# When weight splits and a difference of x are made at the end of an opening block, in an FNet and GLU kernel

## The chip, the core and the metric

The kernel runs on one core of a Trainium2 chip. TensorE (PE) multiplies matrices, VectorE (DVE) and ScalarE (ACT) work on elements, GpSimd (POOL) issues the storing transfers here and does a few tiny operations, SyncE (SP) issues the loading transfers. Each engine takes its instructions in the order in which they are written. The metric is the device time of one execution in microseconds; the median of several executions is compared.

## The reference

`x` is 2048 x 512 (S x D), F is 1792.

```python
xn = layernorm(x)                                # over D
a = xn @ dft_hid_re.T;  b = xn @ dft_hid_im.T
s = dft_seq_re @ a - dft_seq_im @ b              # real part of a 2-D DFT
h = sigmoid(xn @ w_gate) * (xn @ w_up)           # 2048 x 1792
g = silu(h @ w_down)
return x + s * g
```

Everything is float32. The kernel keeps that accuracy by splitting each operand into two float32r parts, hi (a rounded copy, made by ACT) and lo (the value less hi, made by DVE); a product is then three matmuls, hi x hi, hi x lo and lo x hi (`mm3`, lines 72 to 75). Every operand of a product thus costs an ACT copy and, after it, a DVE subtraction (`split`, lines 68 to 70) before TensorE may use it.

## The kernel before

The F dimension is taken in seven groups `g` of 256, the rows of x in two halves `h` of 1024. For a half and a group the gate and up products are made by a scheme of seven products with sums of quarters (Strassen's, in Winograd's form) in place of eight: products 1, 2, 3 and 4 use plain quarters on one side or both, the others use sums on both. The products run in the order 1, 5, 2, 6, 7, 4, 3, and each is one unit of the list `units`: 12 matmuls 128x512 per product, and in some units 12 more (bank `pd`) for the down projection of the group before. `xop[h, k]` is the x operand of product k and `w[k]` the weight operand, both as hi and lo. For product 5 the weight operand is the sum `s1` and the x operand is `x_sum(h, 1)`, a difference of two transposed blocks; for product 6 the weight operand is `s2`, made from `s1`, and the x operand is `x_sum(h, 2)`, made from the first difference. `x_sum(h, 3)` and `x_sum(h, 4)` serve products 7 and 4.

The first group of the first half (h = 0, g = 0) is not done so. It is the opening block, `start` (line 504): its eight plain products run in `chunk(q, f)`, q = 0 to 3 outside and f = 0, 1 inside, while the eight tiles of x are still normalised, turned by TensorE (`turn`) and split (`keep_hi` on ACT, `keep_lo` on DVE) or kept plain (`keep_raw` on ACT). A chunk is 24 matmuls of 256 columns, eight each on hi x hi, and the two mixed pairs. `next_tile(7)`, the last tile, stands inside chunk (2, 1), and chunk (3, 0) is the first that uses it. `gated(b, f)` makes a gated value from two finished banks (ACT sigmoid line 544, DVE multiply line 545); the function it returns, kept in `left`, splits that value one chunk later. Behind the opening block come the units: unit 0 is product 1 of group 1, unit 1 product 5 with, after it, the first down projection of the opening block, for which the weights `w_down[0]` are split in two parts; unit 2 is product 2 and unit 3 product 6.

The order is written out by hand. The opening block calls `units[n][0][1].get()` for n = 0 to 3 (line 624), which makes and splits the weights of products 1, 5, 2 and 6 ahead of their units, one each in chunks (1, 1), (2, 0), (2, 1) and (3, 0). From unit 0 on, the main loop (lines 974 to 986) asks for the operands of a unit two units ahead (`SPLIT_AHEAD`) and for loads five units ahead; `sooner` and `after` hang further work in front of a unit or behind it.

All of it lives in 53 buffers named `page`. A buffer is given again once its last reader is through, so a load into a page waits for whoever used that page before. SP issues its loads in order: a load that waits holds the next ones.

Of the kernel before, what the change touches and what calls it, by code (L numbers as in the profile page):

```python
# [32 lines left out]
def fnet_glu_kernel(ctx: ExitStack, tc: tile.TileContext, x, x_t, c_re, c_im, w_h, w_gu, w_down, out):  # L33
# [9 lines left out]
    def page(shape, dtype=F32R):  # L43
        return pages.tile([P, *shape], dtype, name="page")

    def bank(tag):
        return banks.tile([P, 512], F32, name=tag, bufs=2 if tag == "pd" else 1)
# [77 lines left out]
    xop = {}  # L125
    xraw = {}
    units = []
# [7 lines left out]
    def after(n, f):  # L135
        extra.setdefault(n, []).append(f)
# [7 lines left out]
    def fetch(i, hold=False):  # L144
        pg = page([2, D], F32)
        if hold:
            nc.vector.memset(pg[:, 0, :1], 0.0)
        for j in range(2):
            xs[i + j] = pg[:, j, :]
            nc.sync.dma_start(xs[i + j], x[(i + j) * P : (i + j + 1) * P, :])  # L150
# [3 lines left out]
    def norm_a(i):  # L154
        st = stat.tile([P, 6], F32, name="st")
        mv = stat.tile([P, 2], F32, name="mv")
        rs = stat.tile([P, 2], F32, name="rs")
        nc.vector.bn_stats(st, xs[i])
        nc.vector.bn_aggr(mv, st)
        mean, scale = mv[:, 0:1], rs[:, 1:2]  # L160
        if i >= KH:
            mean, scale = (moments[:, m, i - KH : i - KH + 1] for m in range(2))
            nc.gpsimd.tensor_scalar(mean, mv[:, 0:1], 0.0, None, op0=ALU.add)
        nc.gpsimd.tensor_scalar(rs[:, 0:1], mv[:, 1:2], EPS, None, op0=ALU.add)
        nc.gpsimd.tensor_tensor(scale, rs[:, 0:1], mhalf, op=ALU.pow)
        st_of[i] = mean, scale

    def norm_b(i):
        mean, scale = st_of.pop(i)
        nc.vector.tensor_scalar(xs[i], xs[i], mean, scale, op0=ALU.subtract, op1=ALU.mult)  # L170
# [30 lines left out]
    def turn(i):  # L201
        turned[i] = bank("pd").rearrange("p (d s) -> p d s", d=ND)
        for d in range(ND):
            nc.tensor.transpose(turned[i][:, d, :], xs[i][:, d * P : (d + 1) * P], ident)
# [5 lines left out]
    def keep_raw(i):  # L210
        keys, at = place(i)
        for j, k in enumerate(keys):
            if k not in xraw:
                xraw[k] = page([2, SB], F32)
            nc.scalar.activation(xraw[k][:, :, at], turned[i][:, 2 * j : 2 * j + 2, :], AF.Copy)

    def keep_hi(i):
        keys, at = place(i)
        for j, (h, _, b) in enumerate(keys):
            k = h, XK[j, b]  # L220
            if xop[k].at is None:
                xop[k].at = page([2, SB]), page([2, SB])
            nc.scalar.activation(xop[k].at[0][:, :, at], turned[i][:, 2 * j : 2 * j + 2, :], AF.Copy)

    def keep_lo(i):
        keys, at = place(i)
        for j, (h, _, b) in enumerate(keys):
            hi, lo = xop[h, XK[j, b]].at
            nc.vector.tensor_tensor(lo[:, :, at], turned[i][:, 2 * j : 2 * j + 2, :], hi[:, :, at].bitcast(F32), op=SUB)
# [3 lines left out]
    def x_sum(h, k):  # L233

        if (h, k) not in xsum:
            xsum[h, k] = page([2, SB], F32)
        a, b = {
            1: lambda: (xraw[h, 0, 1], xraw[h, 0, 0]),
            2: lambda: (xraw[h, 1, 1], xsum[h, 1]),
            3: lambda: (xraw[h, 1, 1], xraw[h, 0, 1]),  # L240
            4: lambda: (xraw[h, 1, 0], xsum[h, 2]),
        }[k]()
        nc.vector.tensor_tensor(xsum[h, k], a, b, op=SUB)
# [260 lines left out]
    def start(h, g):  # L504

        loads = [Load(w_gu[g, k], [2, 4 * P]) for k in range(2)]
        wdl = Load(w_down[g], [2, D])
        wd = [Parts([wdl], lambda f=f: wdl.load()[:, f, :], [D], joint=True) for f in range(2)]
        w, ps = {}, {}
        job = Ready(h, g, wd)  # L510

        def w_hi(f, j):
            k, o = QUAD[f, j]
            both = page([2, 4 * P])
            w[f, j] = both[:, 0], both[:, 1]
            nc.scalar.activation(both[:, 0], loads[k].load()[:, o, :], AF.Copy)

        def w_lo(f, j):
            k, o = QUAD[f, j]
            nc.vector.tensor_tensor(w[f, j][1], loads[k].load()[:, o, :], w[f, j][0].bitcast(F32), op=SUB)  # L520

        def chunk(q, f, order, between=None):
            b, a = divmod(q, 2)
            if a == 0:
                for m in range(2):
                    ps[b, f, m] = bank("gu"[m] + ("bc", "ab")[b][f])
            at = slice(a * 2 * P, (a + 1) * 2 * P)
            for n, (u, v) in enumerate(order):
                if n and n - 1 in (between or {}):
                    between[n - 1]()  # L530
                for j, m, k in itertools.product(range(2), repeat=3):
                    d, o = 2 * j + k, (2 * m + k) * P
                    nc.tensor.matmul(
                        ps[b, f, m][:, at],
                        w[f, j][u][:, o : o + P],
                        xop[h, XK[j, b]].at[v][:, k, at],
                        start=n == d == a == 0,
                        stop=n == 2 and d == ND - 1,
                        skip_group_check=True,
                    )  # L540

        def gated(b, f):
            s = page([SB], F32)
            nc.scalar.activation(s, ps[b, f, 0], AF.Sigmoid)
            nc.vector.tensor_mul(s, s, ps[b, f, 1])

            def fin():
                v = job.hs[f, b] = Parts([], lambda: s, [SB], joint=True)
                v.get()

            return fin

        def begin():
            idle = bank("gc")

            def busy(times, wide):
                for _ in range(times):
                    nc.tensor.matmul(idle[:, :wide], ones[:, :P], ones[:, :wide], start=True, stop=True)

            busy(10, 512)  # L560
            fetch(0)
            loads[0].load()
            norm_a(0)
            fetch(2, hold=True)
            loads[1].load()
            norm_a(1)
            w_hi(0, 0)
            norm_b(0)
            turn(0)
            busy(2, 256)  # L570
            keep_hi(0)
            norm_b(1)
            turn(1)
            busy(4, 256)
            keep_hi(1)
            w_hi(0, 1)
            w_lo(0, 0)
            norm_a(2)
            for i in (4, 6):
                fetch(i, hold=True)  # L580
            for n in range(4):
                units[n][0][1].load()
            wdl.load()
            w_lo(0, 1)
            for i in range(2):
                keep_lo(i)
            w_hi(1, 0)
            w_hi(1, 1)
            norm_b(2)
            for i in range(2):  # L590
                keep_raw(i)
            norm_a(3)
            w_lo(1, 0)
            w_lo(1, 1)
            norm_b(3)

            def next_tile(i):
                if i >= KH:
                    return
                turn(i)  # L600
                keep_hi(i)
                if 3 < i + 1 < KH - 1:
                    norm_b(i + 1)
                keep_lo(i)
                if i + 2 < KH:
                    norm_a(i + 2)
                keep_raw(i)

            left = None
            for q in range(4):  # L610
                for f in range(2):
                    if f == 0:
                        chunk(q, f, ((0, 0), (1, 0), (0, 1)))
                        next_tile(2 * q + 2)
                    else:
                        chunk(q, f, ((0, 0), (0, 1), (1, 0)), {int(q == 0): lambda: next_tile(2 * q + 3)})
                    if left:
                        left()
                    left = gated(q // 2, f) if q % 2 else None
                    if (q, f) == (1, 1):  # L620
                        norm_b(KH - 1)
                    n = 2 * q + f - 3
                    if 0 <= n < 4:
                        units[n][0][1].get()
            left()
            x_sum(h, 1)
            x_sum(h, 2)
            after(0, lambda: x_sum(h, 3))
            after(0, lambda: x_sum(h, 4))

        return job, begin

# [312 lines left out]
    with tc.manual_schedule():  # L945
# [3 lines left out]
        for h in range(NH):  # L949
            for g in range(1 - h, NG):  # L950
                job = block(h, g, job, Seven(h, g) if h else Plain(h, g))
            if h == 0:
                n = len(units)
# [85 lines left out]
```

## Time and profile before

| | |
|---|---|
| runs shown | 825.22, 827.76 and 1164.65 us, median 827.76 us |
| profiled execution, own time | 823.7 us |
| its span, first to last instruction | 821.9 us |
| PE busy | 808.8 us, 98% of the span |
| DVE, ACT, POOL busy | 77%, 59%, 18% |
| mean granted TensorE clock | 0.997 |

The span leaves 1.8 us of the profiled execution's time outside it. The run of 1164.65 us is far from the other two, which lie 2.5 us apart. In the rows of the timeline a line number such as L69 is the line of a helper, so operations are told apart by their place in the order: L69 and L70 are the two halves of every split, L223, L229 and L215 are `keep_hi`, `keep_lo` and `keep_raw`, L121 is a sum of weights, L243 an `x_sum`, L533 a chunk's matmul.

### The profile page before, as it was taken

What the parts mean: (1) busy time and instruction counts of PE and PEld (TensorE: products, weight loads), DVE (VectorE), ACT (ScalarE), POOL (GpSimd) and SP (SyncE); (2) the same over time, 40 slices, a digit from 0 to 9 for tenths busy, and PEclk for the clock granted to TensorE, in tenths of its full rate; (3) what the DMA queues carried; (4) which work ended last, traced back from release to release, by engine and by line L of the source; (5) the groups of instructions that cost most, each with busy time, mean ns of one, the idle gap of its engine ahead of it and who ended that gap; (6) DMA issues with size and microseconds to landing.
All of it is one profiled execution on the core that took longest, in us unless ns stands there. A gap on an engine that the chain in (4) does not pass through costs nothing.

```text
span 821.9 us, 10340 instructions
## 1 busy us (share of the span) xinstructions
PE 808.8 (98%) x3654; PEld 671.5 (82%) x3654; DVE 636.5 (77%) x792; ACT 486.4 (59%) x740; POOL 147.5 (18%) x222
## 2 busy tenths in 40 slices
PE   9889999999999999999999999999999999999997
PEld 7868888888888888888888888888888888888786
DVE  6768668768878767766788797889888976997946
ACT  4555555556676787787787774444354545535441
POOL 3123552121111221212121110011101110002201
PEclk9999999999999999999999999999999999999999
DMA  8247999996767899999999897458937994799984
GB/s 298 86 158 274 221 323 254 336 274 170 221 147 209 241 231 246 247 194 228 272 292 303 185 359 281 147 205 306 315 145 286 333 393 152 250 323 399 312 265 77
DMA packets 58660, 204.64 MB, mean 249 GB/s; under 512 B 6640, under 2 KB 6896, under 8 KB 58608
## 3 DMA queue, kind: packets, MB, share of 16 engines
q0 software_dynamic: 24624, 85.48, 41.2%
q1 hardware_dynamic: 33984, 118.50, 40.9%
q8 instruction: 28, 0.46, 0.2%
q14 instruction: 24, 0.20, 0.1%
HBM read 121.63 MB, written 85.99 MB: 253 GB/s over the span
## 4 chain that ended last, share of the span: by engine, by line
PE 94%; DVE 3%; ACT 1%; issue 1%; POOL 0%; DVEq 0%
PE pd L73 6%; PE pd L75 6%; PE pd L74 6%; PE ga L73 5%; PE ua L73 5%; PE ga L74 5%; PE ua L74 5%; PE ua L75 5%; PE ga L75 5%; PE gc L74 3%; PE uc L73 3%; PE gc L75 3%; PE uc L74 3%; PE uc L75 3%; PE gc L73 3%; PE gb L74 3%
## 5 line engine op out<-in xcount | busy, mean ns | idle before, releaser
L70 DVE TENSOR_TENSOR page<-page 128x1024 fp32r<-128x1024 f32 (+1 forms) x362 | 340.5, 969 | 134.4 <-ACT page L69 133.4
L69 ACT ACTIVATE page<-page 128x1024 fp32r<-128x1024 f32 (+1 forms) x362 | 291.4, 853 | 112.1 <-DVE page L121 77.4
L121 DVE TENSOR_TENSOR page<-page 128x1024 f32<-128x1024 f32 (+2 forms) x184 | 169.3, 934 | 1.9 <-PE ua L74 1.4
L302 ACT ACTIVATE page<-pd 128x512 f32<-128x512 f32 x154 | 90.6, 597 | 85.1 <-PE pd L75 78.5
L306 POOL DMA_DIRECT2D g_part<-page x69 | 60.5, 911 | 271.2 <-ACT page L302 169.6
L73 PE MATMUL pd<-page 128*128 128x512 f32 x242 | 94.3, 389 | 0.8 <-DVE page L883 0.8
L75 PE MATMUL pd<-page 128*128 128x512 f32 x242 | 94.2, 389 | 0.0
L74 PE MATMUL pd<-page 128*128 128x512 f32 x242 | 94.1, 389 | 0.0
L73 PE MATMUL ga<-page 128*128 128x512 f32 x200 | 78.0, 390 | 0.0
L74 PE MATMUL ga<-page 128*128 128x512 f32 x200 | 77.8, 389 | 0.0
L73 PE MATMUL ua<-page 128*128 128x512 f32 x200 | 77.8, 389 | 0.0
L75 PE MATMUL ga<-page 128*128 128x512 f32 x200 | 77.8, 389 | 0.0
L74 PE MATMUL ua<-page 128*128 128x512 f32 x200 | 77.8, 389 | 0.0
L75 PE MATMUL ua<-page 128*128 128x512 f32 x200 | 77.8, 389 | 0.0
L73 PEld LDWEIGHTS pd<-page 128*128 128x128 f32 x242 | 45.4, 188 | 10.6 <-issue 1.2
L75 PEld LDWEIGHTS pd<-page 128*128 128x128 f32 x242 | 45.4, 188 | 9.5
L74 PEld LDWEIGHTS pd<-page 128*128 128x128 f32 x242 | 45.4, 188 | 9.4
L73 PE MATMUL gc<-page 128*128 128x512 f32 x124 | 48.6, 392 | 2.3 <-ACT page L69 2.3
L74 PE MATMUL gc<-page 128*128 128x512 f32 x124 | 48.6, 392 | 0.8 <-DVE page L70 0.8
L73 PE MATMUL ub<-page 128*128 128x512 f32 (+1 forms) x126 | 48.3, 383 | 0.5 <-DVE page L925 0.5
L73 PE MATMUL uc<-page 128*128 128x512 f32 x124 | 48.7, 393 | 0.0
L75 PE MATMUL gc<-page 128*128 128x512 f32 x124 | 48.6, 392 | 0.0
(130 smaller groups left out, 1314.1 us busy)
## 6 DMA issues: line engine op xcount, KB each, us to landing
g_part<-page POOLq DMA_DIRECT2D x77, 512.0 KB, 9.0
page<-f_part SPq DMA_DIRECT2D x36, 512.0 KB, 5.7
page<-in_c_re_dram SPq DMA_DIRECT2D x34, 512.0 KB, 6.4
page<-in_c_im_dram SPq DMA_DIRECT2D x33, 512.0 KB, 6.8
page<-in_w_gu_dram SPq DMA_DIRECT2D x28, 512.0 KB, 6.5
f_part<-page POOLq DMA_DIRECT2D x28, 512.0 KB, 6.6
page<-in_w_down_dram SPq DMA_DIRECT2D x14, 512.0 KB, 7.1
page<-xn_part SPq DMA_DIRECT2D x14, 512.0 KB, 8.0
```

What stands on the lines that cost most here:

```text
L69: nc.scalar.activation(hi, src, AF.Copy)
L70: nc.vector.tensor_tensor(lo, src, hi.bitcast(F32), op=SUB)
L73: nc.tensor.matmul(ps, ws[0], ms[0], start=first, stop=False, skip_group_check=go_on)
L74: nc.tensor.matmul(ps, ws[0], ms[1], start=False, stop=False, skip_group_check=go_on)
L75: nc.tensor.matmul(ps, ws[1], ms[0], start=False, stop=last, skip_group_check=go_on)
L121: (engine or nc.vector).tensor_tensor(dst, a, b, op=op)
L302: nc.scalar.activation(pg[:, o, :], po, AF.Copy, scale=float(sign))
L306: nc.gpsimd.dma_start(g_part[i], pg, accum_op=ADD)
```

## The change

```diff
                     else:
                         chunk(q, f, ((0, 0), (0, 1), (1, 0)), {int(q == 0): lambda: next_tile(2 * q + 3)})
+                    if (q, f) == (3, 0):
+                        x_sum(h, 1)
+                    if (q, f) == (3, 1):
+                        xop[h, 5].get()
                     if left:
                         left()
                     left = gated(q // 2, f) if q % 2 else None
@@
                     n = 2 * q + f - 3
                     if 0 <= n < 4:
-                        units[n][0][1].get()
+                        units[(0, 2, 1, 3)[n]][0][1].get()
             left()
-            x_sum(h, 1)
             x_sum(h, 2)
             after(0, lambda: x_sum(h, 3))
-            after(0, lambda: x_sum(h, 4))
+            after(1, lambda: x_sum(h, 4))
```

The weights of product 2, which are plain, are split in chunk (2, 0), and those of product 5, a sum, in chunk (2, 1): the two change places. The first difference of x is made after chunk (3, 0) and split after chunk (3, 1), ahead of the gated value (1, 0); before, it was made after the last gated value was split, and its split stood in unit 0. The fourth difference moves from the end of unit 0 to the end of unit 1. No operation is added or taken away, and TensorE's order stays as it is.

On ACT, from the split of the gated value (0, 1) on, the order before is this. page_181 and page_183 hold the plain weights of group 1, page_447 their sums; page_400, page_516 and page_550 are gated values.

```order
L69 ACTIVATE page_444<-page_400 128x512
L69 ACTIVATE page_449<-page_447 128x512 [waits DVE_49]
L223 ACTIVATE page_331<-pd_462 128x2x128 [waits PE_49]
L223 ACTIVATE page_334<-pd_462 128x2x128
L215 ACTIVATE page_347<-pd_462 128x2x128 [waits DVE_49]
L215 ACTIVATE page_349<-pd_462 128x2x128
L69 ACTIVATE page_489<-page_181 128x512
L544 ACTIVATE page_516<-ga_407 128x512 [waits PE_49]
L69 ACTIVATE page_520<-page_447 128x512 [waits DVE_49]
L69 ACTIVATE page_547<-page_516 128x512
L544 ACTIVATE page_550<-gb_452 128x512 [waits PE_49]
L69 ACTIVATE page_553<-page_550 128x512 [waits DVE_49]
```

The row behind these is the split of the first difference of x, 128x1024. In the changed kernel, where page_487 holds the sums, page_516 the first difference and page_518 and page_556 the gated values, the same stretch reads:

```order
L69 ACTIVATE page_444<-page_400 128x512
L69 ACTIVATE page_447<-page_181 128x512
L223 ACTIVATE page_331<-pd_460 128x2x128 [waits PE_49]
L223 ACTIVATE page_334<-pd_460 128x2x128
L215 ACTIVATE page_347<-pd_460 128x2x128 [waits DVE_49]
L215 ACTIVATE page_349<-pd_460 128x2x128
L69 ACTIVATE page_489<-page_487 128x512 [waits DVE_49]
L544 ACTIVATE page_518<-ga_407 128x512 [waits PE_49]
L69 ACTIVATE page_522<-page_487 128x512 [waits DVE_49]
L69 ACTIVATE page_549<-page_516 128x1024
L69 ACTIVATE page_553<-page_518 128x512
L544 ACTIVATE page_556<-gb_450 128x512 [waits PE_49]
```

The copy that waits for DVE's sum stands behind the last tile's `keep_hi` and `keep_raw` instead of ahead of them, and the copy of the first difference stands ahead of the last two gated values.

On DVE, from the multiply of the gated value (1, 0) on, before; page_185 is `w_down[0]`:

```order
L545 TENSOR_TENSOR page_516<-page_516,ua_408 128x512
L121 TENSOR_TENSOR page_447<-page_447,page_181 128x512
L70 TENSOR_TENSOR page_520<-page_447,page_520 128x512
L70 TENSOR_TENSOR page_547<-page_516,page_547 128x512
L545 TENSOR_TENSOR page_550<-page_550,ub_453 128x512
L70 TENSOR_TENSOR page_553<-page_550,page_553 128x512
L243 TENSOR_TENSOR page_556<-page_347,page_197 128x1024
L243 TENSOR_TENSOR page_558<-page_349,page_556 128x1024
L70 TENSOR_TENSOR page_561<-page_556,page_560 128x1024
L70 TENSOR_TENSOR page_564<-page_185,page_564 128x512
L70 TENSOR_TENSOR page_567<-page_185,page_567 128x512
```

and in the changed kernel, from the first difference on:

```order
L243 TENSOR_TENSOR page_516<-page_347,page_197 128x1024
L545 TENSOR_TENSOR page_518<-page_518,ua_408 128x512
L121 TENSOR_TENSOR page_487<-page_487,page_181 128x512
L70 TENSOR_TENSOR page_522<-page_487,page_522 128x512
L70 TENSOR_TENSOR page_550<-page_516,page_549 128x1024
L70 TENSOR_TENSOR page_553<-page_518,page_553 128x512
L545 TENSOR_TENSOR page_556<-page_556,ub_451 128x512
L70 TENSOR_TENSOR page_559<-page_556,page_559 128x512
L243 TENSOR_TENSOR page_562<-page_349,page_516 128x1024
L70 TENSOR_TENSOR page_564<-page_185,page_564 128x512
L70 TENSOR_TENSOR page_567<-page_185,page_567 128x512
```

The lo part of the first difference (page_561 before, page_550 now) is written five places sooner against the gated values, and the two splits of `w_down[0]` stay last in the row, right behind the second difference.

Since pages are given out in the order in which they come free, some loads get another page than before. SP's loads of the later tiles of x and of the weights that follow wait before for this:

```order
L150 DMA page_773<-in_x_dram 128x512 [waits DMAHW4_49,DMAHW2_49,DVE_49]
L150 DMA page_773<-in_x_dram 128x512 [waits DMAHW3_49]
L84 DMA page_780<-in_w_down_dram 128x1024 [waits DVE_49]
L150 DMA page_870<-in_x_dram 128x512 [waits DMAHW5_49,DMASW2_49,DVE_49]
L150 DMA page_870<-in_x_dram 128x512 [waits DMAHW6_49]
```

and in the changed kernel, where a DMASW is a transfer that POOL issued, for this:

```order
L150 DMA page_773<-in_x_dram 128x512 [waits DMAHW2_49,DVE_49,Activation_49]
L150 DMA page_773<-in_x_dram 128x512 [waits DMAHW3_49]
L84 DMA page_780<-in_w_down_dram 128x1024 [waits DMAHW4_49,DVE_49]
L150 DMA page_870<-in_x_dram 128x512 [waits DMASW5_49,DMAHW5_49,DMASW4_49,PE_49]
L150 DMA page_870<-in_x_dram 128x512 [waits DMAHW6_49]
```

The load of tiles 10 and 11 (page_870) now takes a page that held tiles 2 and 3 of x, which POOL stores to `xn_part` behind the first down projection's result; before, it took a page that DVE's weight sums had used.

## Prediction

> **What bounds the kernel now.** I read the page first: which engine is busy, and whose work makes up the chain that ended last.
>
> ```profile
> PE 808.8 (98%) x3654; PEld 671.5 (82%) x3654; DVE 636.5 (77%) x792; ACT 486.4 (59%) x740; POOL 147.5 (18%) x222
> PE 94%; DVE 3%; ACT 1%; issue 1%; POOL 0%; DVEq 0%
> ```
>
> TensorE is the bound: it is idle for 821.9 - 808.8 = 13.1 us in all. The change leaves its instructions as they are, so it can only win idle time, or time at a lower clock. The list of what TensorE waited for over the whole run (us in total, times, longest) says where that is.
>
> ```profile
> PE gc L73 <- ACT page L69: 2.3, 1, 2.3
> PE ga L533 <- ACT page L223: 2.1, 1, 2.1
> PE gc L558 <- DVE ones L52: 1.4, 1, 1.4
> PE pd L73 <- DVE page L883: 0.8, 1, 0.8
> PE gc L74 <- DVE page L70: 0.8, 1, 0.8
> PE ub L73 <- DVE page L925: 0.5, 1, 0.5
> PE pd L204 <- DVE page L170: 0.3, 1, 0.3
> ```
>
> The first, second and fifth row fall in the stretch touched; L52 and L170 belong to the start, L883 and L925 to the hidden transform at the very end. TensorE's timeline around those three (start, us, operation, idle before):
>
> ```profile
> 29.81 0.40 PE L533 MATMUL ub<-page 128*128 128x256 f32 x2
> 32.31 0.50 PE L533 MATMUL ga<-page 128*128 128x256 f32 x2 [2.10 <-ACT page L223]
> ...
> 38.17 0.40 PE L73 MATMUL ga<-page 128*128 128x512 f32 x1
> ...
> 40.69 0.39 PE L75 MATMUL ua<-page 128*128 128x512 f32 x1
> 43.43 0.50 PE L73 MATMUL gc<-page 128*128 128x512 f32 x1 [2.35 <-ACT page L69]
> 44.73 0.50 PE L74 MATMUL gc<-page 128*128 128x512 f32 x1 [0.80 <-DVE page L70]
> ...
> 48.95 0.40 PE L73 MATMUL pd<-page 128*128 128x512 f32 x1
> ...
> 51.69 0.39 PE L73 MATMUL gb<-page 128*128 128x512 f32 x1
> ```
>
> The first stop is chunk (3, 0), which lacks the hi part of the last tile. The second and third are product 5 (bank gc), which lacks first the hi and then the lo part of the first difference. The rest of product 5 is slow besides. The 12 pd matmuls after it start at 48.95 and the next product at 51.69: 2.74 us, 0.23 each. From 44.73 to 48.95 stand 11 matmuls of product 5, which at that pace take 2.5 us and took 4.22: 1.7 us lost. The windows show the cause (length, then busy us of PE, PEld, DVE, ACT and POOL, granted clock, DMA share, GB/s):
>
> ```profile
> 41.00:45.00 4.00, 0.85 (x3) 0.46 (x3) 3.97 (x5) 2.68 (x5) 0.00 (x0) 1.00 0.01 2
> 45.00:48.40 3.40, 3.40 (x9) 2.58 (x9) 3.40 (x5) 1.35 (x2) 0.00 (x0) 0.52 0.44 126
> 49.00:60.00 11.00, 11.00 (x50) 9.11 (x49) 5.65 (x7) 6.41 (x10) 3.44 (x5) 1.00 0.64 209
> ```
>
> After a stretch in which TensorE was busy 0.85 of 4 us, the granted clock is 0.52 for 3.4 us, and full again after that. Meanwhile DVE is busy all the time: it is the engine that TensorE waits for here.
>
> **Part 1: the two weight splits change places.** ACT and DVE before the first stop:
>
> ```profile
> 29.36 0.63 ACT L69 ACTIVATE page<-page 128x512 fp32r<-128x512 f32 x1
> 31.36 0.63 ACT L69 ACTIVATE page<-page 128x512 fp32r<-128x512 f32 x1 [1.36 <-DVE page L121]
> 31.89 0.64 ACT L223 ACTIVATE page<-pd 128x256 fp32r<-128x256 f32 x2
> ...
> 37.20 1.15 ACT L69 ACTIVATE page<-page 128x512 fp32r<-128x512 f32 x2 [1.36 <-DVE page L121]
> 38.26 0.58 ACT L544 ACTIVATE page<-gb 128x512 f32<-128x512 f32 x1
> 30.64 0.68 DVE L121 TENSOR_TENSOR page<-page 128x512 f32<-128x512 f32 x1
> 32.63 0.75 DVE L229 TENSOR_TENSOR page<-pd,page 128x256 fp32r<-128x256 f32 x2
> ```
>
> At 31.36 ACT copies product 5's weights after 1.36 us of waiting for DVE's sum, and the last tile's keep_hi (31.89) is queued behind. The copy that takes its place needs nothing of DVE; its weights are in the same load as product 1's, split long before. Two such copies in a row put the next instruction 38.26 - 37.20 = 1.06 us on, 0.53 each. So keep_hi starts at 29.36 + 1.06 = 30.42, 1.47 sooner. TensorE started 0.42 behind it (32.31 - 31.89) and so starts at 30.84: 0.63 of the stop of 2.10 stays. The bounds are 0 and 2.10; I take 1.47, all from rows. Product 1 then starts at 36.70, and product 5 could start at 40.69 + 0.23 - 1.47 = 39.45.
>
> The displaced sum now runs on DVE behind keep_lo, at about 31.8 (32.63 - 1.47 + 0.75, less 0.1 of overlap), and its split ends about 33.9. Product 5 is 5 us away: this costs nothing.
>
> **Part 2: the first difference, made and split sooner.** The rows of the engines that make it (the 42.32 row is one copy of 1024 and two of 512, so the first takes 2.10 - 1.06 = 1.04; the 43.46 row likewise on DVE, 1.2 and twice 0.6):
>
> ```profile
> 35.25 0.60 ACT L544 ACTIVATE page<-ga 128x512 f32<-128x512 f32 x1 [0.66 <-PE ga L533]
> 42.32 2.10 ACT L69 ACTIVATE page<-page 128x1024 fp32r<-128x1024 f32 x3 [1.89 <-DVE page L243]
> 40.45 0.69 DVE L70 TENSOR_TENSOR page<-page 128x512 fp32r<-128x512 f32 x1 [0.70 <-ACT page L69]
> 41.06 2.48 DVE L243 TENSOR_TENSOR page<-page 128x1024 f32<-128x1024 f32 x2
> 43.46 2.42 DVE L70 TENSOR_TENSOR page<-page 128x1024 fp32r<-128x1024 f32 x3
> 53.47 1.83 DVE L70 TENSOR_TENSOR page<-page 128x1024 fp32r<-128x1024 f32 x2 [3.58 <-ACT page L69]
> ```
>
> Before, two differences (41.06 to 43.54) stand in front of the lo part, and ACT's copy waits for the first of them. In the new order I step DVE and ACT forward with these durations, 0.6 for an operation of 512, 1.2 for one of 1024, and 0.7 for each pass through ACT in between (its 0.63 and the hand-over). x_sum 1 runs on DVE from 33.8 to 35.0. The multiply of gated (1, 0), whose sigmoid comes at 35.25 - 1.47 = 33.8, follows until 35.7: it is put off by some 0.6 us, but unit 0 needs bank ua only at 38.1. Then product 6's sum until 36.3, ACT's copy until 36.95, its lo part until 37.65. ACT's copy of the difference, queued behind that copy, ends at 37.9. DVE's lo part runs from 37.95 to 39.15. TensorE wants hi at 39.45 and lo one matmul later, at 39.68. Both are there, lo with 0.5 us to spare. So product 5 runs without a stop.
>
> What that is worth: before, product 5 took from 40.92 (40.69 + 0.23) to the first pd matmul at 48.95, 8.03 us, against 2.73 for 12 matmuls at full clock. The sum of 5.30 is 3.6 of stops and 1.7 of low clock. The lower clock I count in full, since it came right behind the stops and the earlier stop of 2.10 alone, between stretches of dense work, brought none: the matmuls from 32.31 to 38.17, two chunks of 24, run at 0.12 each, half the 0.23 for half the columns.
>
> [...] The sum with the clock restored is 5.8, and 4.1 if the slow stretch stayed.
>
> **Part 3: what is late next.** Behind the difference, the remaining work on DVE is: lo of gated (1, 0) until 39.75; multiply of gated (1, 1) until 40.4; a pass through ACT; its lo part until 41.75; x_sum 2 until 42.9; then the two lo parts of w_down[0], until 43.55 and 44.15. The pd matmuls now start at 39.45 + 2.73 = 42.18, and the third of them, the first that reads a lo weight, is due at 42.64. It waits until 43.6: a new stop of 1.0 us. (Before, these splits were over at 45.9, 3 us ahead of pd.) Its bounds: 0, if DVE's steps come closer together, and 2.0, if each of the ten steps costs 0.1 more. I take 1.0, the sum of the rows. A stop of 1.0 is shorter than the one of 2.10 that brought no lower clock.
>
> Behind that nothing is late. The second difference is split on ACT soon after x_sum 2 ends at 42.9 and on DVE by about 47.0; product 6 follows pd and product 2 at 48.7. x_sum 4, now behind unit 1, runs until 48.2 and serves product 4, two units later still. DVE has room there: before, it stands idle for 3.58 us up to 53.47.
>
> **The sum:** 1.47 + 5.30 - 1.0 = 5.8 us. All later units keep their distances, since their loads, splits and stores are tied to units and the list has no wait of TensorE's between 45 us and the hidden transform. The profiled execution takes 823.7 - 5.8 = 817.9 us (span 816.1). The runs shown, 825.22 and 827.76, average 826.5, 2.8 above the profiled one; from there the sum gives 820.7, and from the median 822.0. I write 820.5.
>
> **The rivals.**
>
> The new stop grows (A). If DVE is 1.4 us later than I have it, the stop at pd is 2.4 and, like 2.35 + 0.80 before, may bring the low clock: 1.4 + 1.7 lost, gain 2.7, 821.0 on the profiled base. For it: ten hand-overs in a row on a DVE without slack. Against it: I stepped with durations of this trace.
>
> The slow clock stays (B), because something other than the stops lowers it: the gain is 5.8 - 1.7 = 4.1, the time 819.6. Against it stands the busy share in the window before. [...]
>
> The change does not reach its aim (C): the lo part of the difference comes after 41 because keep_raw or the weight sum is later than I have it. The stops move by what part 1 wins and no more: 823.7 to 822.
>
> Slower (D): the load of tiles 10 and 11, which now waits for POOL's stores of tiles 2 and 3.
>
> ```profile
> 53.32 2.90 POOL L197 DMA_DIRECT2D xn_part<-page  x4
> 55.92 0.82 SPq L150 DMA_DIRECT2D page<-in_x_dram  x2
> 79.33 0.69 DVE L158 BATCH_NORM_STATS2 st<-page 128x6 f32<-128x512 f32 x1
> DMA to landing us min/median/max: 2.9/7.6/11.5
> ```
>
> The four stores are issued from 53.32 to 56.22, now 5.8 sooner, until 50.4; the slowest landing seen, 11.5, gives 61.9, plus 4 for the load, 66. DVE's first use of tile 10 moves from 79.33 to 73.5: 7.5 us to spare. From 73.5 on each us of delay stops DVE, and TensorE once its two units of split work are used up, 5.5 us later. With the load landing at 87, TensorE stands 8 us and loses 1.7 to the clock: 817.9 + 9.7 = 827.6. Nothing in these rows comes near that.
>
> **How the numbers follow.** Forecast 0.70; A 0.12; B 0.07; C 0.08; D 0.03. On the two bases the forecast lies between 817.9 and 822.0, and with the bounds of the pd stop (one us either way) between 816.9 and 823.0. From the median A reaches 825.1, and C 826.3 and above. The range 815.5 to 826.5 takes in the forecast, B, A and most of C and leaves out D; below, it has 1.4 for a pd stop of 0 with part 1 winning more than its 1.47. Two per cent, about what a measurement of this kernel can tell from no change, is 16.6 us, more than all the idle time of TensorE: faster by that 0.01, slower 0.02, within it 0.97.
>
> **What would show it.** In the profile of the changed kernel: TensorE's wait for keep_hi at about 0.6 instead of 2.1 (part 1); no wait on bank gc and a granted clock of 1.0 between 40 and 50 us (part 2); one new wait of about 1 us of a pd matmul for DVE L70 (part 3); the first pd matmul near 42.2. A wait on gc of over 1 us says C; a pd wait over 2 with a slow stretch after it says A; a slow stretch without such a wait says B; idle time of DVE before L158 near 73 says D. I am wrong altogether if the span does not fall by 3 us or more.

## The result and the profile after

The changed kernel takes 819.87 us (median of 12 runs, 817.73 to 824.56), the kernel before 825.3 us (median of 12, with the one at 1164.65 among them). The ratio is 0.9934, with a 95% interval of 0.9911 to 0.9957: faster by 5.4 us, which is within 2%, and right where the forecast put it (820.5, range 815.5 to 826.5). The profiled execution took 817.99 us with a span of 816.2; the sum had given 817.9 and 816.1. The forecast of 820.5 stood for a gain of 5.8 us on a kernel before of 826.3; that one came out 1.0 us lower and the gain 0.4 us smaller, so part of the closeness of the medians is chance.

What TensorE waited for in the changed kernel, over the whole run (us in total, times, longest); the lines are three further on than before, so L886 and L928 are the L883 and L925 of the hidden transform:

```profile
PE gc L558 <- DVE ones L52: 1.4, 1, 1.4
PE pd L73 <- DVE page L886: 0.8, 1, 0.8
PE pd L75 <- DVE page L70: 0.8, 1, 0.8
PE ga L533 <- ACT page L223: 0.6, 1, 0.6
PE ub L73 <- DVE page L928: 0.5, 1, 0.5
```

Both rows in which product 5 (L73 and L74 on bank gc) waited are gone; the gc row that is left, L558, belongs to the start. The 2.1 of the last tile's hi part is 0.6, and one row is new: a pd matmul that waits for DVE. The timeline of TensorE shows them in their places (start, us, operation, idle before):

```profile
30.78 0.50 PE L533 MATMUL ga<-page 128*128 128x256 f32 x2 [0.63 <-ACT page L223]
36.63 0.40 PE L73 MATMUL ga<-page 128*128 128x512 f32 x1
39.38 0.39 PE L73 MATMUL gc<-page 128*128 128x512 f32 x1
39.60 0.39 PE L74 MATMUL gc<-page 128*128 128x512 f32 x1
...
42.09 0.39 PE L73 MATMUL pd<-page 128*128 128x512 f32 x1
42.32 0.39 PE L74 MATMUL pd<-page 128*128 128x512 f32 x1
43.51 0.50 PE L75 MATMUL pd<-page 128*128 128x512 f32 x1 [0.80 <-DVE page L70]
...
45.90 0.39 PE L73 MATMUL gb<-page 128*128 128x512 f32 x1
```

Product 5 (39.38 to 42.09) runs in 2.71 us, where it took 8.03. DVE's own timeline tells why, and why the third pd matmul waits:

```profile
31.85 0.68 DVE L121 TENSOR_TENSOR page<-page 128x512 f32<-128x512 f32 x1
33.84 1.22 DVE L243 TENSOR_TENSOR page<-page 128x1024 f32<-128x1024 f32 x1
37.90 1.83 DVE L70 TENSOR_TENSOR page<-page 128x1024 fp32r<-128x1024 f32 x2 [0.26 <-ACT page L69]
39.65 0.68 DVE L545 TENSOR_TENSOR page<-page,ub 128x512 f32<-128x512 f32 x1
41.03 0.69 DVE L70 TENSOR_TENSOR page<-page 128x512 fp32r<-128x512 f32 x1 [0.70 <-ACT page L69]
41.64 1.22 DVE L243 TENSOR_TENSOR page<-page 128x1024 f32<-128x1024 f32 x1
42.77 1.29 DVE L70 TENSOR_TENSOR page<-page 128x512 fp32r<-128x512 f32 x2
```

The lo part of the first difference starts at 37.90 (the row joins it with the next split) and is done by about 39.1, half a microsecond ahead of the matmul at 39.60. The lo parts of w_down[0] start at 42.77, behind the second difference, and the first of them ends near 43.4: the third pd matmul starts at 43.51 instead of 42.55, 0.96 late. The windows of the changed kernel (length, busy us of PE, PEld, DVE, ACT, POOL, granted clock, DMA share, GB/s) show the clock:

```profile
41.00:45.00 4.00, 3.20 (x15) 2.33 (x14) 3.97 (x5) 3.24 (x6) 0.00 (x0) 1.00 0.26 73
45.00:48.40 3.40, 3.40 (x17) 2.82 (x16) 3.40 (x5) 2.63 (x5) 1.41 (x3) 1.00 0.75 260
```

It is 1.00 where it was 0.52, and 17 matmuls stand in the 3.4 us that held 9.

### The profile page after: what moved, and what is told of

Its sections match the earlier page's. It is cut to its first block, busy times and chain, and to the rows that moved or that the text cites. A ratio compares the mean times of both kernels' runs of the same rounds, so it can differ in the third digit from the quotient of the medians.

```text
span 816.2 us, 10340 instructions
## 1 busy us (share of the span) xinstructions
PE 807.0 (99%) x3654; PEld 670.6 (82%) x3654; DVE 636.6 (78%) x792; ACT 486.1 (60%) x740; POOL 147.6 (18%) x222
## 4 chain that ended last, share of the span: by engine, by line
PE 94%; DVE 3%; ACT 1%; DMA 1%; issue 1%; POOL 0%; SPq 0%; DVEq 0%
PE pd L75 7%; PE pd L73 7%; PE pd L74 6%; PE ga L73 5%; PE ga L74 5%; PE ua L75 5%; PE ua L73 5%; PE ga L75 5%; PE ua L74 5%; PE gc L74 3%; PE gb L75 3%; PE gb L74 3%; PE uc L73 3%; PE uc L75 3%; PE uc L74 3%; PE gc L73 3%
## 5 line engine op out<-in xcount | busy, mean ns | idle before, releaser
L73 PE MATMUL pd<-page 128*128 128x512 f32 x242 | 94.3, 390 | 0.8 <-DVE page L886 0.8
L74 PE MATMUL pd<-page 128*128 128x512 f32 x242 | 94.2, 389 | 0.0
L73 PE MATMUL ga<-page 128*128 128x512 f32 x200 | 78.0, 390 | 0.0
L74 PE MATMUL ga<-page 128*128 128x512 f32 x200 | 77.9, 390 | 0.0
L73 PE MATMUL ua<-page 128*128 128x512 f32 x200 | 77.9, 389 | 0.0
L74 PE MATMUL ua<-page 128*128 128x512 f32 x200 | 77.9, 389 | 0.0
L73 PEld LDWEIGHTS pd<-page 128*128 128x128 f32 x242 | 45.4, 188 | 10.6 <-issue 1.2
L74 PEld LDWEIGHTS pd<-page 128*128 128x128 f32 x242 | 45.4, 188 | 9.3
L73 PE MATMUL ub<-page 128*128 128x512 f32 (+1 forms) x126 | 48.3, 383 | 0.5 <-DVE page L928 0.5
L74 PE MATMUL gc<-page 128*128 128x512 f32 x124 | 48.3, 389 | 0.0
L73 PE MATMUL uc<-page 128*128 128x512 f32 x124 | 48.3, 389 | 0.0
L75 PE MATMUL uc<-page 128*128 128x512 f32 x124 | 48.3, 389 | 0.0
L74 PE MATMUL uc<-page 128*128 128x512 f32 x124 | 48.3, 389 | 0.0
```

What stands on the lines that cost most here:

```text
L73: nc.tensor.matmul(ps, ws[0], ms[0], start=first, stop=False, skip_group_check=go_on)
L74: nc.tensor.matmul(ps, ws[0], ms[1], start=False, stop=False, skip_group_check=go_on)
L75: nc.tensor.matmul(ps, ws[1], ms[0], start=False, stop=last, skip_group_check=go_on)
```

## Experiments

The theory: three separate terms, +1.47 from the swap of the weight splits, +5.30 from the early difference (3.6 of stops and 1.7 of a low clock that the stops bring), and -1.0 for a new stop which is just the length of DVE's queue. The rivals: that a part is worth nothing by itself because the next stop swallows it, that the low clock has another cause, and that the fourth difference's move is needed too. The start of the program moves by some tenths of a microsecond (the first matmul of chunk (3, 0) stands at 32.31 and 31.93 in the two profiles of the kernel before, at 30.78 and 30.38 in the first two of the changed one), so the stops are also compared by their distance from that matmul.

**Part 1 alone.**

```diff
-                        units[n][0][1].get()
+                        units[(0, 2, 1, 3)[n]][0][1].get()
```

> Only part 1: the splits of the weights of products 2 and 5 change places, the differences of x stay as before. Theory (the two parts add up): TensorE's first stop falls from 2.1 to 0.6 us; everything DVE does behind it moves with it, so product 5 still stops for about 3.1 us in two pieces (2.4 and 0.8), 1.5 us earlier than before; span 820.4 us with the low clock after the stops, 818.7 without it. Rival (the first stop only hides in the second): product 5 starts at 43.4 as before, span 821.9.

Measured: span 820.6 us; 823.4 us against 824.26, ratio 0.9984 (0.9957 to 1.001), which by itself would not be told from nothing. The timeline tells it:

```profile
30.45 0.50 PE L533 MATMUL ga<-page 128*128 128x256 f32 x2 [0.63 <-ACT page L223]
41.55 0.50 PE L73 MATMUL gc<-page 128*128 128x512 f32 x1 [2.35 <-ACT page L69]
42.86 0.50 PE L74 MATMUL gc<-page 128*128 128x512 f32 x1 [0.81 <-DVE page L70]
```

The first stop is 0.63, and product 5 starts 11.10 us behind the chunk, as before (43.43 - 32.31 = 11.12). Nothing is swallowed: the 1.47 stays, because DVE's queue ahead of product 5 moves with the last tile. Behind these stops, too, stands a stretch near half clock (windows as above):

```profile
40.70:44.10 3.40, 1.74 (x6) 1.23 (x7) 3.40 (x5) 3.40 (x6) 0.00 (x0) 1.00 0.01 2
44.10:47.50 3.40, 3.40 (x9) 2.65 (x8) 3.40 (x4) 0.38 (x1) 0.00 (x0) 0.50 0.72 202
```

Of the ten executions of this kernel the shortest, 820.79 us with a span of 819.0, has a mean granted clock of 1.000. A stretch of 3.4 us at half clock takes 0.002 off the mean, so this one had none, and its span is near the 818.7 that was expected without the low clock. Its stops are not on record; if they were the same, the slow stretch does not follow them every time.

**Part 2 alone**, the changed kernel with the old order of the weight splits:

```diff
-                        units[(0, 2, 1, 3)[n]][0][1].get()
+                        units[n][0][1].get()
```

> Only part 2: the first difference of x made and split early, the fourth later, the weight splits in the old order. Theory: the first stop stays at 2.1 us, product 5 runs without a stop and at full clock from 40.9, a stop of about 1 us appears at the third matmul of the down projection; the gain is 5.3 - 1.0 = 4.3, span 817.6 us. Rival (the difference is only in time because the swap freed ACT and DVE): a stop of over 0.5 us at product 5, span 818.5 or more.

Measured: 820.35 us against 824.26, ratio 0.995 (0.993 to 0.9971), 3.9 us. Its waits of TensorE:

```profile
PE ga L533 <- ACT page L223: 2.1, 1, 2.1
PE ga L73 <- ACT page L452: 1.5, 1, 1.5
PE gc L558 <- DVE ones L52: 1.4, 1, 1.4
PE pd L73 <- DVE page L886: 0.8, 1, 0.8
PE pd L75 <- DVE page L70: 0.7, 1, 0.7
PE ub L73 <- DVE page L928: 0.5, 1, 0.5
```

Product 5 does not stop, without the swap too; the rival falls. The span is 819.2, 1.6 more than expected, and 1.5 of that is the second row, a stop near 146 us, far behind the change, of which more below. The two parts add up: 1.3 (820.6 against 821.9) and 4.2 (819.2 less that 1.5, against 821.9) are 5.5, the whole change 5.7 by its spans. The medians give 0.9 and 3.9 against 5.4, with intervals too wide to test the sum.

**The fourth difference left where it was.**

```diff
-            after(1, lambda: x_sum(h, 4))
+            after(0, lambda: x_sum(h, 4))
```

> The change with the fourth difference of x left behind unit 0 where it was. Theory: it puts 1.1 us of DVE work ahead of the lo part of product 6, which the changed kernel has 1.7 us before TensorE wants it; nothing stops, span 816.2 us as with the whole change. Rival (this part of the change is needed): a new stop at product 6, up to 1 us, span 816.5 to 817.2.

Measured: one execution, 818.42 us, span 816.6. The span lies in the range that the rival gives, but TensorE's waits in this stretch are those of the changed kernel and no other: the stop at product 6 that the rival needs is not there. Of the 0.4 us above the changed kernel's span, 0.3 is a wait at the start of the program (pd, L204, for DVE's L170). On DVE the two differences now stand together and the lo part of product 6 starts a microsecond later, at 46.79 against 45.71:

```profile
43.92 2.35 DVE L243 TENSOR_TENSOR page<-page 128x1024 f32<-128x1024 f32 x2
46.19 0.68 DVE L121 TENSOR_TENSOR page<-page 128x512 f32<-128x512 f32 x1
46.79 2.95 DVE L70 TENSOR_TENSOR page<-page 128x1024 fp32r<-128x1024 f32 x3
```

It ends near 48.0, and TensorE wants it at about 48.6. So this part of the change buys nothing that this execution shows; it keeps 1.1 us of distance.

**The new stop made longer.** The third difference ahead of the splits of w_down[0], then the third and the fourth; each puts 1.13 us more of DVE work in front of them.

```diff
             x_sum(h, 2)
-            after(0, lambda: x_sum(h, 3))
+            x_sum(h, 3)
             after(1, lambda: x_sum(h, 4))
```

> The change with the third difference of x made right behind the second, ahead of the splits of w_down[0], instead of behind unit 0: 1.13 us more on DVE in front of them. Theory (the remaining stop is the length of DVE's queue ahead of the lo part of w_down[0]): the stop at the third pd matmul grows from 0.8 to 1.9 us, the granted clock stays at 1.0 as after the 2.1 us stop of the kernel before; span 817.3 us. Rival (the low clock comes with stops in this place): the 1.9 us stop is followed by 3.4 us at half clock, span 819.0 us.

```diff
             x_sum(h, 2)
-            after(0, lambda: x_sum(h, 3))
-            after(1, lambda: x_sum(h, 4))
+            x_sum(h, 3)
+            x_sum(h, 4)
```

> The change with the third and the fourth difference of x made right behind the second, ahead of the splits of w_down[0]: 2.27 us more on DVE in front of them. Theory: the stop at the third pd matmul grows from 0.8 to 3.1 us in one piece. If it is TensorE's idle time that lowers the clock, as 2.35 + 0.80 us did before, a stretch of 3.4 us near half clock follows or not, by where it falls; span 818.5 us without it, 820.2 with it. Rival (the slow stretch before had another cause): full clock in any case, span 818.5.

Measured, one execution each: spans 817.0 and 820.0. The stops with the third alone, and with both:

```profile
30.41 0.51 PE L533 MATMUL ga<-page 128*128 128x256 f32 x2 [0.64 <-ACT page L223]
44.28 0.50 PE L75 MATMUL pd<-page 128*128 128x512 f32 x1 [1.93 <-DVE page L70]
```

```profile
30.56 0.50 PE L533 MATMUL ga<-page 128*128 128x256 f32 x2 [0.63 <-ACT page L223]
45.56 0.50 PE L75 MATMUL pd<-page 128*128 128x512 f32 x1 [3.07 <-DVE page L70]
```

From the chunk to the late matmul it is 12.73 us in the changed kernel (43.51 - 30.78), 13.87 with one more difference and 15.00 with two: 1.14 and 1.13 apiece, the length of one difference on DVE. So the new stop is DVE's queue and nothing else. The stop of 1.93 leaves the clock at full speed (1.00 from 44.3 to 47.7 us). The one of 3.07 does not, as the windows of that kernel show:

```profile
43.40:46.80 3.40, 1.24 (x5) 1.04 (x6) 3.40 (x6) 0.35 (x2) 0.00 (x0) 1.00 0.82 242
46.80:50.20 3.40, 3.40 (x9) 2.61 (x8) 1.05 (x1) 1.61 (x3) 0.12 (x1) 0.51 0.16 66
50.20:60.00 9.80, 9.80 (x44) 8.07 (x43) 5.19 (x7) 6.82 (x12) 4.42 (x7) 1.00 0.79 259
```

The slow stretch follows the stop to a place where the changed kernel has none: 3.4 us at 0.51. It costs, by the span, 820.0 - 816.2 - 2.27 = 1.5 us. The rival that the slow stretch had another cause falls.

**Both kernels again.** No edit.

> The kernel before, unchanged, profiled a second time. Theory (the low clock follows from the stops at product 5): the same stops of 2.1, 2.35 and 0.8 us and again a stretch near half clock of 3.4 us, unless it falls elsewhere; span 821.9 us, or 820.2 if the clock stays full this time. Rival (the slow stretch is an accident of one execution): the stops without any low clock in most executions.

> The changed kernel, unchanged, profiled a second time. Theory: stops of 0.6 us at the last tile and 0.8 us at the third pd matmul, full clock between 30 and 60 us, span 816.2 us; where the span is longer, the extra time stands outside this stretch, as it must in the runs of 820 to 824 us. Rival: the extra time of the longer runs is lost in this stretch, by a later DVE.

Measured: the kernel before has a span of 822.6, the same stops (2.10, 2.35, 0.81) and again a stretch at half clock, this time from 44.0 to 47.4, with TensorE busy 0.59 of the 3.4 us ahead of it:

```profile
40.60:44.00 3.40, 0.59 (x2) 0.19 (x1) 3.37 (x4) 2.07 (x4) 0.00 (x0) 1.00 0.01 2
44.00:47.40 3.40, 3.05 (x7) 2.47 (x8) 3.40 (x5) 1.97 (x4) 0.00 (x0) 0.50 0.15 57
```

The 0.7 us that it has on the first profile come with a stop of 0.96 at 150 us. The changed kernel has a span of 815.8 and the stops expected, 0.64 and 0.79. It was a short execution, so it does not tell where the longer ones lose their time.

**What is left to win.** The splits of w_down[0] ahead of the last gated value's, and both weight splits behind the last tile, the sum's first:

```diff
-                        units[(0, 2, 1, 3)[n]][0][1].get()
+                    for i in ((0,), (), (1, 2), (3,))[n] if 0 <= n < 4 else ():
+                        units[i][0][1].get()
+            for v in job.wd:
+                v.get()
             left()
             x_sum(h, 2)
```

> The change, and two steps more: the splits of w_down[0] are made ahead of the split of the last gated value, where ACT and DVE stand idle, and the two weight splits that changed places are both made behind the last tile, the sum's first. Theory: the stop of 0.8 us at the third pd matmul goes (lo of w_down[0] at about 41 against 42), the stop of 0.6 us at the last tile's hi part falls to 0.1; span 814.6 us. Rival (DVE becomes late for product 5 instead, since its lo part is at 39.1 and TensorE now there at 38.9 to 39.1): a stop of up to 0.3 us there, span 814.9; if the stops only move on, 816.2.

Measured: 816.7 us against 823.5, ratio 0.991 (0.9893 to 0.9926), span 814.7. Between the start and the hidden transform TensorE has no listed wait left:

```profile
PE gc L558 <- DVE ones L52: 1.4, 1, 1.4
PE pd L73 <- DVE page L888: 0.8, 1, 0.8
PE ub L73 <- DVE page L930: 0.5, 1, 0.5
PE pd L204 <- DVE page L170: 0.3, 1, 0.3
```

Of the rival's stop at product 5 only 0.1 us is there: its second matmul starts 0.32 us behind the first (38.29 and 38.61), where 0.23 is the pace.

On DVE the splits of w_down[0] take the place of the idle time in which it waited for ACT's copy of the last gated value (0.70 in the changed kernel): the row that starts at 39.67 joins them with that value's lo part, and the first pd matmul is only at 41.24.

```profile
39.08 0.68 DVE L545 TENSOR_TENSOR page<-page,ub 128x512 f32<-128x512 f32 x1
39.67 1.89 DVE L70 TENSOR_TENSOR page<-page 128x512 fp32r<-128x512 f32 x3
41.48 2.36 DVE L243 TENSOR_TENSOR page<-page 128x1024 f32<-128x1024 f32 x2
```

Beside the changed kernel on one chip:

> The changed kernel, unchanged, timed beside the next one on the same chip. Theory: stops of 0.6 and 0.8 us in the stretch touched, span 816.2 us; executions that take longer lose their time near 145 us, where ACT waits for transfers, as in two profiles so far. Ratio to the kernel before 0.993.

> The change with the splits of w_down[0] ahead and both weight splits behind the last tile, timed beside the changed kernel. Theory: 1.4 to 1.5 us less than the changed kernel, span 814.7, ratio to the kernel before 0.991. Rival (its five close times so far were the chip's, not the kernel's): the median within 1 us of the changed kernel's.

Measured: 818.34 us (817.49 to 820.0) and 816.78 us (816.6 to 817.01), ratios 0.9925 (0.9906 to 0.9944) and 0.99 (0.9883 to 0.9918) to the same runs of the kernel before. The two intervals overlap, but the five times of the one lie below the six of the other, and the difference of the medians is 1.6 us where the two stops add up to 1.4. This version is the fastest of the three.

## Why the prediction was right

Part 1: keep_hi was put at 30.42 and TensorE's start at 30.84; they came at 30.34 and 30.78 (the whole program ran 0.06 earlier), with 0.63 of the stop left, as worked out. Run alone, the swap leaves the same stop of 0.63, and its span is 1.3 us shorter than before; its median would not show it.

Part 2: the lo part of the difference was stepped to 37.95 and came at 37.90; product 5 did not stop. The 5.30 was made of 3.6 of stops and 1.7 of low clock, and the second piece was the less certain, since it rested on one execution. It is borne out in the profiles: each of the three that have stops of 2.35 and 0.8 there has the slow stretch (the third is the swap alone), and behind the stop of 3.07 at pd the clock was 0.51. The execution of the swap alone at a clock of 1.000 says that it may be missing in some. For the kernel before no such execution is on record: of the 34 that were timed beside the experiments none has a mean clock above 0.998, while of the twelve of the changed kernel seven have 0.999 or 1.000.

In all four profiles that have it the low clock, 0.50 to 0.52, lasts 3.4 us. TensorE did not stand still for so long before it: no gap ahead of a slow stretch was longer than 3.07 us, and TensorE was busy 0.59, 0.77, 1.24 and 1.74 of the 3.4 us ahead of the four.

Part 3: the stop at the third pd matmul was put at 1.0 and delayed it by 0.96; the profile lists 0.80 of that as idle, since the matmul before it is counted busy for 0.39 where its place in the row is 0.23. Rival A, with this stop at 2.4 and a low clock, did not occur; beside it stand a stop of 1.93, which cost no more than its own length, and one of 3.07, which cost 1.5 us more, in one execution each. The prediction took the old stop of 2.10 as a length that brings no low clock. In the three profiles that have it the clock is 1.00 behind it, but that its length is the reason is not shown, as the last section says; the stop of 0.80 that came left the clock at 1.00.

Rival D was priced too high. The load of tiles 10 and 11 went out at 51.92, 4.0 us sooner than before (55.92), though it now waits for a store, and DVE's first use of tile 10 came at 73.54 without a wait:

```profile
47.53 2.90 POOL L197 DMA_DIRECT2D xn_part<-page  x4
51.92 0.82 SPq L150 DMA_DIRECT2D page<-in_x_dram  x2
73.54 0.69 DVE L158 BATCH_NORM_STATS2 st<-page 128x6 f32<-128x512 f32 x1
```

I had taken the slowest landing of all those stores, 11.5 us, which belongs to the ones issued from 96.9 us on. The four awaited here had landed within 3.3 to 4.6 us in the kernel before, and did so within 3.3 to 3.7 in the changed one.

One sentence of the prediction holds for the profiled execution only: that TensorE waits nowhere between 45 us and the hidden transform. Two of the later profiles have a stop near 146 to 150 us.

## What to carry to other kernels

Here an operand that ACT copies and DVE completes held what was queued behind it: ACT stood 1.36 us for DVE's sum with the last tile's hi part next in its queue. So at a narrow place the copies that wait for nothing go first, and the operand that TensorE wants next goes ahead of results wanted later. Step the two queues forward with durations of the trace before changing the order: here it gave the stop that stayed and the stop that was new to a tenth of a microsecond; the new one stands where the displaced work went. Count a stop of the matrix engine by more than its idle time when it is long: here the stops of 2.35 and 0.8 one after the other, and the one of 3.07, also cost 1.7 and 1.5 us of half clock, while single stops of 0.80, 1.93 and 2.10 left the clock at 1.00.

## What the runs showed of the hardware

TensorE's busy time in a stretch of 3.4 us at the stops named, and the granted clock in the 3.4 us behind it:

| profile | stops (us) | stretch (us) | TensorE busy (us) | clock in the next 3.4 us |
|---|---|---|---|---|
| kernel before, second profile | 2.35, 0.81 | 40.60 to 44.00 | 0.59 | 0.50 |
| kernel before | 2.35, 0.80 | 41.60 to 45.00 | 0.77 | 0.52 |
| both differences ahead | 3.07 | 43.40 to 46.80 | 1.24 | 0.51 |
| swap alone | 2.35, 0.81 | 40.70 to 44.10 | 1.74 | 0.50 |
| kernel before | 2.10 | 28.90 to 32.30 | 1.31 | 1.00 |
| third difference ahead | 1.93 | 40.90 to 44.30 | 1.47 | 1.00 |
| changed kernel | 0.80 | 40.50 to 43.90 | 2.60 | 1.00 |

The stop of 2.10 left the clock at 1.00 in the second profile of the kernel before and in that of part 2 alone as well. The busy time does not draw the line: 1.31 and 1.47 left the clock at 1.00, and 1.74 was followed by 0.50. Nor does idle time alone: at the end of the program the last matmul of the kernel before ends at 817.29 and the clock falls at 819.98, 2.7 us later, while in the changed kernel the last one ends at 811.49 and the clock is still 1.00 at the end of the span, 4.7 us later. What decides it these runs do not show.

The stop near 146 us, which I had not expected, may be one of transfers; no run tests that. In the profile of part 2 alone, TensorE and ACT there (idle before, and what ended it, "issue" where the profile shows nothing that did):

```profile
146.65 0.50 PE L73 MATMUL ga<-page 128*128 128x512 f32 x1 [1.51 <-ACT page L452]
```

```profile
145.49 0.63 ACT L69 ACTIVATE page<-page 128x512 fp32r<-128x512 f32 x1 [4.21 <-issue]
```

The row of ACT behind this one is L452 at 146.02, which empties the bank that TensorE wants. What ended ACT's wait this profile does not name; POOL issued two stores to `xn_part` from 129.50 on. In the kernel before, the wait of ACT at the same split, 2.72 us, is put down to such a store, issued at 129.5, which landed 16.7 us later; in the changed kernel the one that this split waits for was issued at 124.1 and landed after 16.9. In the second profile of the kernel before TensorE starts at 150.15 after 0.96 of idle time, again waiting for L452, and the longest wait of ACT at a split between 100 and 170 us is 4.5. A long wait of ACT is not enough by itself: in the changed kernel ACT stands for 4.19 us ahead of the same split, which starts at 142.32, and TensorE does not stop.

The stop shows in the kernel before (0.96) and in part 2 alone (1.51), so the change does not bring it. Whether it makes the spread of the changed kernel's times, 817.73 to 824.56, is open: none of its three profiles, with spans of 815.8 to 816.2, was one of the long executions. The longest one has a mean granted clock of 0.995, where the eight shortest have 0.998 or more, so some of its time went at a low clock, in a place that is not on record.
